# A second Strassen level for two of the seven products of an MLP's second matmul

## Chip, cores, metric

One Trainium2 chip, one core. The metric is the device time of one execution in microseconds (us), the median of several.

## The reference

```python
B, S, D, F = 1, 2048, 1024, 3584            # bf16 inputs
def reference(x, w1, b1, w2, b2):
    y = _layernorm(x, axis=-1)
    h = _gelu(jnp.einsum("bsd,df->bsf", y, w1) + b1)      # first matmul
    return jnp.einsum("bsf,fd->bsd", h, w2) + b2          # second matmul
```

## The kernel before

Tokens are worked in two blocks of 1024. In each, both matmuls are done by one level of Strassen's method (Winograd's form): operands are cut into quarters, seven products of quarters replace eight, and sums of quarters are made on VectorE (DVE). The program is made by a small list scheduler: it places every operation on its engine by an assumed cost and a priority, and so fixes each engine's in-order instruction stream before the kernel runs.

In the second matmul the quarters of `h` are A11 to A22 (512 tokens by 1792 of K), those of `w2` are B11 to B22 (1792 by 512 columns). S and T are sums of them. One product is four token tiles, each of 14 matmuls (128 of K, 128 tokens, 512 columns).

```python
SEQ2 = (1, 2, 5, 3, 6, 7, 4)
hold = {1: hb, 6: hb, 7: hb, 4: hb, 2: h2, 5: h5, 3: h5}     # PSUM banks, four each
...
def prods(p, a, b):
    first = prev[p] is None
    for t in range(TH):                                      # 4 token tiles
        fn = [(lambda e, k=k, t=t: e.matmul(
            ps[:, hold[p][t].k, :], lhsT=a[0][:, k, t * P:(t + 1) * P], rhs=b[0][:, k, :],
            start=(first and k == 0), stop=(k == NU - 1), skip_group_check=True), a[1][k] + b[1][k])
            for k in range(NU)]                              # 14 matmuls of 512 columns
        ...
        if p in (1, 5, 6):
            keep(p, t, 0 if p == 1 else 1, at)               # bank + bias -> SBUF (fp32)
        if p == 2:
            final(2, t, 11, 1, at, (h2[t],))                 # bank + kept 1 -> output quarter 11
        if p == 6:
            final(3, t, 12, 6, at + 1, (h5[t],))
        if p == 7:
            final(7, t, 22, 5, at, ())
        if p == 4:
            final(4, t, 21, None, at, (hb[t],))              # bank + bias -> output quarter 21
...
S1 = sums(s, h[21], A[21], A[22], ALU.add, (), pt[2], "hS1")
T1 = sums(s, w2q16[12], B[12], B[11], ALU.subtract, (), pt[2] + 4, "wT1")
prods(1, A[11], B[11])
S2 = sums(...)
prods(2, A[12], B[21])
...                                                          # products 5, 3, 6, 7 and their sums
prods(4, A[22], T4)
```

Of the kernel before, what the change touches and what calls it, by code (L numbers as in the profile page):

```python
# [23 lines left out]
P = 128  # L24
HT = 512
# [9 lines left out]
MM512 = 0.2163  # L35
MM256 = 0.1085
# [8 lines left out]
class Op:  # L45
# [3 lines left out]
    def __init__(self, engs, cost, fn, deps, prio, name, sem=None, inc=1, nbytes=None, alloc=None, frees=()):  # L49
# [3 lines left out]
        self.sem, self.inc, self.nbytes, self.alloc, self.frees = sem, inc, nbytes, alloc, frees  # L53
# [20 lines left out]
class Planner:  # L74
# [12 lines left out]

    def place(self):
# [12 lines left out]
        while left:  # L101
            best = None
            for e in self.ENGS:
                cands = []
                t0 = 1e9
                for o in avail:
# [3 lines left out]
                    if o.alloc is not None:  # L110
                        fr = o.alloc.pool.free
                        if not fr:
                            continue
                        rel = fr[0][1]
                        if rel is not None:
                            r = max(r, rel.end + LAT)
# [15 lines left out]
            if o.alloc is not None:  # L132
                k, rel = o.alloc.pool.free.pop(0)
                o.alloc.k = k
                if rel is not None:
                    o.deps.append(rel)
            c = o.cost[e] if isinstance(o.cost, dict) else o.cost
# [59 lines left out]
def bass_standalone__mixer_channel_mlp__prompt_kernel(  # L197
# [24 lines left out]
    with ExitStack() as es:  # L222
# [25 lines left out]
        x16 = x_sb[:, :, :].bitcast(FP16)  # L248
        h = {q: h_sb[:, n] for n, q in enumerate((11, 12, 21, 22))}
        w2a16 = w2a_sb[:, :, :, :].bitcast(FP16)  # L250
# [21 lines left out]
        T_MM2 = TH * 7 * NU * MM512  # L272
# [314 lines left out]
        KG = [(k, min(k + 2, NU)) for k in range(0, NU, 2)]  # L587
        w2_free = {}
        stores = []
        SLOT2 = NU * MM512  # L590
        SEQ2 = (1, 2, 5, 3, 6, 7, 4)

        def sums(s, dst, a, b, op, deps, prio, name):

            res = []
            for g, (k0, k1) in enumerate(KG):
                dl = list(deps)
                for k in range(k0, k1):
                    dl += a[1][k] + b[1][k]
                o = add("DVE", 0.63, lambda e, k0=k0, k1=k1: e.tensor_tensor(  # L600
                    out=dst[:, k0:k1, :], in0=a[0][:, k0:k1, :], in1=b[0][:, k0:k1, :], op=op),
                    list(dict.fromkeys(dl)), prio + 0.3 * g, f"{name}_{s}_{g}")
# [3 lines left out]
        def flat(a):  # L606
            return list(dict.fromkeys(o for l in a[1] for o in l))

        def mm2_block(s):
            t0 = base2[s]  # L610
            pt = {p: t0 + k * TH * SLOT2 for k, p in enumerate(SEQ2)}
            m2, rd, sn = {}, {}, {}
            hb = [Holder(banks) for _ in range(TH)]
            h2 = [Holder(banks) for _ in range(TH)]
            h5 = [Holder(banks) for _ in range(TH)]
            hold = {1: hb, 6: hb, 7: hb, 4: hb, 2: h2, 5: h5, 3: h5}
            prev = {1: None, 2: None, 5: None, 6: 1, 7: 6, 4: 7, 3: 5}
# [3 lines left out]
            def done(p):  # L621
                return [m2[(p, t)] for t in range(TH)]

            def evac(p, t, dst, in1, deps, name, at, alloc, frees):
                return add("DVE", 0.69, lambda e: e.tensor_tensor(out=dst(), in0=ps[:, hold[p][t].k, :], in1=in1(),  # L625
                                                                  op=ALU.add), [m2[(p, t)], *deps], at,
                           f"{name}_{s}_{t}", alloc=alloc, frees=frees)
# [3 lines left out]

            def keep(p, t, d, at):
                hs = sn[(p, t)] = Holder(snaps)
                rd[(p, t)] = evac(p, t, lambda: sn_sb[:, hs.k, :], bias(d), (b2_ld,), f"r{p}", at, hs, ())

            def final(p, t, q, add_p, at, frees):
                ho = Holder(outs)
                r = (s * NT + (q // 10 - 1) * TH + t) * P
                c = (q % 10 - 1) * HT
                if add_p is None:  # L640
                    in1, deps = bias(0), (b2_ld,)
                else:
                    hs = sn[(add_p, t)]
                    in1, deps, frees = (lambda: sn_sb[:, hs.k, :]), (rd[(add_p, t)],), (hs, *frees)
                f = rd[(p, t)] = evac(p, t, lambda: o_sb[:, ho.k, :], in1, deps, f"o{q}", at, ho, frees)
# [4 lines left out]
            def prods(p, a, b):  # L650
                first = prev[p] is None
                for t in range(TH):
# [12 lines left out]
                    if p == 2:  # L665
                        final(2, t, 11, 1, at, (h2[t],))
# [129 lines left out]
```

## Time and profile before

| | before |
|---|---|
| median of 3 runs | 357.11 us (356.89 to 358.32) |
| span of the profiled run | 355.3 us |
| TensorE (PE) busy | 347.8 us, 98% |
| VectorE (DVE) busy | 236.1 us, 66% |
| granted TensorE clock, mean | 0.999 |

PE is busy 98% of the span. This alone proves little: the Trainium skill, Perfetto Trace Analysis, "Identifying the Most-Contended Engine", says that matmul busy time is no good measure of headroom. Stronger evidence is that the chain of waits, followed back from the end, never leaves PE in the body. These are its pieces from the first second-matmul block on (start, length, what; "x49" are recorded matmuls, of which a few per cent are missing):

```profile
98.63 10.74 PE ps L653 x49
...
109.42 10.74 PE ps L653 x49
...
120.21 14.62 PE ps L653 x67
...
183.18 84.61 PE ps L533 x392
...
267.84 10.74 PE ps L653 x49
...
314.89 37.52 PE ps L653 x173
352.41 0.02 issue
352.44 0.69 DVE o_sb L625
```

The second-matmul block from 267.84 to 352.44 is 84.6 us for 392 matmuls: 215.9 ns each, with no stall. The next view, the busy table by windows, takes product 1, product 2 and the whole second block. Its columns are the window, its length, then busy us (and instructions) of PE, weight loads, DVE, ScalarE and GpSimd, then clock, DMA share and GB/s:

```profile
98.60:110.70 12.10, 12.02 (x55) 5.46 (x56) 5.06 (x8) 1.03 (x2) 0.00 (x0) 1.00 1.07 346
110.70:122.80 12.10, 12.05 (x56) 5.47 (x56) 9.42 (x17) 0.00 (x0) 0.00 (x0) 1.00 0.23 73
267.90:352.40 84.50, 84.29 (x387) 38.02 (x390) 48.60 (x77) 0.94 (x2) 0.00 (x0) 1.00 0.21 67
```

DVE is busy 5.06 of 12.1 us in product 1, 9.42 in product 2 and 48.60 of 84.5 us in the block, so there seems to be room. The timeline of PE in the head (start, length, line, operation, count) becomes important later:

```profile
6.50 1.03 PE L401 MATMUL ps<-ident,x_sb 128*128 128x128 f16 x8 [2.50 <-DVE x_sb L363]
8.11 1.86 PE L495 MATMUL ps<-yw_sb,w_sb 128*128 128x128 f16 x16 [0.58 <-ACT yw_sb L408]
9.77 0.72 PE L401 MATMUL ps<-ident,x_sb 128*128 128x128 f16 x8
10.32 1.06 PE L495 MATMUL ps<-yw_sb,w_sb 128*128 128x128 f16 x16
```

Eight 128-column matmuls (transposes) take 1.03 us, then 0.72; sixteen take 1.86 us, then 1.06. The array starts at half its clock here: eight like them take 0.62 us later in the head. The mean of 0.999 and the sliced clock row of the page do not show it, because they count the time before the first clock record of the trace as full clock. The first full-width products on `t1` operands start at 28.48 us.

### The profile page before, as it was taken

The numbers are of one execution on the slowest core, as the hardware profiler recorded it, in microseconds if no ns is written. First come the engines' busy times: TensorE is split into PE (matmuls) and PEld (weight loads), VectorE is DVE, ScalarE is ACT, GpSimd is POOL, SyncE is SP. The second block draws the span as 40 slices with busy tenths as digits, with TensorE's granted clock in tenths as the row PEclk, the third lists the DMA queues.
The fourth block names the chain that finished last, engine by engine and source line by source line (L and its number), as shares of the span: only waits on it lengthen the run. The fifth ranks groups of instructions, "written<-read, shape, count | busy, mean of one in ns | idle before, by whom it ended". The sixth has DMA issues, their size and how long they took to land.

```text
span 355.3 us, 4675 instructions
## 1 busy us (share of the span) xinstructions
PE 347.8 (98%) x1833; PEld 168.5 (47%) x1843; DVE 236.1 (66%) x395; ACT 125.7 (35%) x202; POOL 12.1 (3%) x31
## 2 busy tenths in 40 slices
PE   5999999999999999999999999999999999999996
PEld 4985444444444444444444444444444444444442
DVE  5789799898847658972716657655542946797222
ACT  4766766577620000000017676667662000000000
POOL 2310000010100000000000000000000000000000
PEclk9999999999999999999999999999999999999999
DMA  7739849643096100155765333030007510001111
GB/s 247 243 58 345 267 118 326 209 118 100 21 316 217 45 14 2 34 114 93 224 220 156 109 118 111 11 117 2 0 1 248 167 44 17 0 0 45 45 44 44
DMA packets 47391, 40.93 MB, mean 115 GB/s; under 512 B 12298, under 2 KB 45322, under 8 KB 47370
## 3 DMA queue, kind: packets, MB, share of 16 engines
q1 hardware_dynamic: 47226, 40.52, 37.2%
q8 instruction: 14, 0.23, 0.3%
q10 hardware_dynamic: 144, 0.13, 0.1%
q14 instruction: 7, 0.06, 0.1%
HBM read 33.82 MB, written 4.19 MB: 107 GB/s over the span
## 4 chain that ended last, share of the span: by engine, by line
PE 97%; DMA 1%; ACT 1%; issue 0%; SPq 0%; DVE 0%
PE ps L653 47%; PE ps L533 44%; PE ps L495 4%; DMA x_sb<-in_x_dram 1%; PE ps L401 1%; ACT h_sb L372 0%; SPq L278 0%; DVE o_sb L625 0%; ACT yw_sb L408 0%; ACT mv_sb L374 0%; PE ps L341 0%
## 5 line engine op out<-in xcount | busy, mean ns | idle before, releaser
L653 PE MATMUL ps<-w2a_sb,h_sb 128*128 128x512 bf16 (+1 forms) x442 | 96.7, 379 | 0.3
L533 PE MATMUL ps<-yw_sb,t_sb 128*128 128x512 f16 x416 | 96.2, 379 | 0.0
L545 ACT COPY sn_sb<-ps 128x512 f32<-128x512 f32 x67 | 39.2, 585 | 105.5 <-PE ps L533 105.5
L533 PE MATMUL ps<-yw_sb,w_sb 128*128 128x512 f16 x312 | 73.9, 379 | 0.0
L653 PE MATMUL ps<-yw_sb,h_sb 128*128 128x512 f16 (+1 forms) x332 | 72.6, 379 | 0.2
L653 PEld LDWEIGHTS ps<-w2a_sb,h_sb 128*128 128x128 f16 x448 | 43.7, 98 | 52.9
L556 ACT ACTIVATE h_sb<-sn_sb,b_sb 128x512 f16<-128x512 f32 x78 | 55.2, 718 | 24.2 <-DVE sn_sb L550 19.9
L533 PEld LDWEIGHTS ps<-yw_sb,t_sb 128*128 128x128 f16 x416 | 40.6, 98 | 49.0
L550 DVE TENSOR_TENSOR sn_sb<-ps,sn_sb 128x512 f32<-128x512 f32 x78 | 52.4, 687 | 14.9 <-PE ps L533 14.2
L653 PEld LDWEIGHTS ps<-yw_sb,h_sb 128*128 128x128 f16 x336 | 32.8, 98 | 39.7
L533 PEld LDWEIGHTS ps<-yw_sb,w_sb 128*128 128x128 bf16 x312 | 30.3, 98 | 36.6
L600 DVE TENSOR_TENSOR h_sb<-h_sb 128x1024 f16<-128x1024 f16 x56 | 35.8, 683 | 2.4 <-ACT h_sb L556 2.4
L625 DVE TENSOR_TENSOR sn_sb<-ps,b_sb 128x512 f32<-128x512 f32 x24 | 16.6, 690 | 25.4 <-PE ps L653 25.4
L625 DVE TENSOR_TENSOR o_sb<-ps,sn_sb 128x512 bf16<-128x512 f32 x24 | 16.6, 691 | 24.7 <-PE ps L653 24.5
L470 DVE TENSOR_TENSOR t_sb<-w_sb,t_sb 128x1024 f16<-128x1024 bf16 x26 | 17.9, 689 | 11.9 <-PE ps L533 11.2
L470 DVE TENSOR_TENSOR t_sb<-w_sb 128x1024 f16<-128x1024 bf16 x26 | 17.8, 683 | 10.6 <-PE ps L533 8.3
L353 DVE BATCH_NORM_STATS2 st_sb<-x_sb 128x6 f32<-128x512 bf16 x26 | 17.3, 679 | 4.4 <-DMA x_sb<-in_x_dram 4.4
L556 ACT ACTIVATE h_sb<-ps,b_sb 128x512 f16<-128x512 f32 x26 | 17.7, 682 | 1.9 <-PE ps L533 1.9
L495 PE MATMUL ps<-yw_sb,w_sb 128*128 128x128 f16 x256 | 16.4, 225 | 0.6 <-ACT yw_sb L408 0.6
L495 PEld LDWEIGHTS ps<-yw_sb,w_sb 128*128 128x128 bf16 x256 | 15.4, 100 | 1.3 <-DMA w_sb<-in_w_dram 0.8
L625 DVE TENSOR_TENSOR o_sb<-ps,b_sb 128x512 bf16<-128x512 f32 x8 | 5.5, 690 | 14.0 <-PE ps L653 14.0
L437 DVE TENSOR_TENSOR yw_sb<-yw_sb 128x1024 f16<-128x1024 f16 x16 | 9.9, 686 | 0.3 <-PE ps L495 0.2
(37 smaller groups left out, 101.8 us busy)
## 6 DMA issues: line engine op xcount, KB each, us to landing
w_sb<-in_w_dram SPq DMA_DIRECT2D x28, 512.0 KB, 5.0
w2a_sb<-in_w_dram SPq DMA_DIRECT2D x4, 1792.0 KB, 8.4
yw_sb<-in_w_dram SPq DMA_DIRECT2D x4, 1792.0 KB, 11.9
out_dram<-o_sb SPq DMA_DIRECT2D x32, 128.0 KB, 1.7
x_sb<-in_x_dram SPq DMA_DIRECT2D x15, 256.0 KB, 8.2
yw_sb<-x_sb SPq DMA_TRANSPOSE x20, 2.5
b_sb<-in_b_dram SPq DMA_DIRECT2D x1, 256.0 KB, 6.4
x_sb<-in_x_dram ACTq DMA_DIRECT2D x1, 128.0 KB, 2.5
```

The costliest lines, as they stand in the source:

```text
L353: st = [add("DVE", 0.68, lambda e, k=k: e.bn_stats(st_sb[:, i, 6 * k:6 * k + 6], x_sb[:, i, k * HT:(k + 1) * HT]), (x_ld[(s, i)][k], *gate ...
L401: fn = [(lambda e, j=j, k=k, hold=hold: e.transpose(out=ps16[:, hold.k, j * P:(j + 1) * P], in_=x16[:, i, k * HT + j * P:k * HT + (j + 1) ...
L437: res.append(add("DVE", 0.64, lambda e, sl=sl: e.tensor_tensor(out=yop[n][:, sl, :], in0=yop[x0][:, sl, :], in1=yop[x1][:, sl, :], op=op), ...
L470: return add("DVE", 0.65, lambda e: e.tensor_tensor(out=tv(k), in0=x0, in1=x1, op=ALU.subtract), [*deps, *war.get(k, ())], prio + 0.5 * k, ...
L495: fn = [(lambda e, b=b, hb=hold[f], f=f, k=k, t=t: e.matmul(ps[:, hb.k, t * P:(t + 1) * P], lhsT=lhs[:, k, f * P:(f + 1) * P], rhs=yop[f"A ...
L533: fn = [(lambda e, k=k: e.matmul(ps[:, hold[p].k, :], lhsT=lhs[:, k, :], rhs=yop[yo][:, k, :], start=(first and k == 0), stop=(k == KH - 1 ...
L545: return e.copy(out=dst, in_=src) if o_.eng == "ACT" else e.tensor_copy(dst, src)
L550: return add("DVE", 0.69, lambda e: e.tensor_tensor(out=sn_sb[:, hold_s.k, :], in0=ps[:, hold[p].k, :], in1=sn_sb[:, hold_s.k, :], op=ALU. ...
L556: r = h_ok[(s, q, u)] = add("ACT", 0.70, lambda e: e.activation(out=h[q][:, u, :], in_=src(), func=ACT.Gelu_apprx_tanh, bias=b1_sb[:, f:f ...
L600: o = add("DVE", 0.63, lambda e, k0=k0, k1=k1: e.tensor_tensor(out=dst[:, k0:k1, :], in0=a[0][:, k0:k1, :], in1=b[0][:, k0:k1, :], op=op), ...
L625: return add("DVE", 0.69, lambda e: e.tensor_tensor(out=dst(), in0=ps[:, hold[p][t].k, :], in1=in1(), op=ALU.add), [m2[(p, t)], *deps], at ...
L653: fn = [(lambda e, k=k, t=t: e.matmul(ps[:, hold[p][t].k, :], lhsT=a[0][:, k, t * P:(t + 1) * P], rhs=b[0][:, k, :], start=(first and k == ...
```

## The change

A12 B21 and A22 T4 each enter one output quarter only (so does product 3, which stays as it was). The change runs each of the two by Strassen's method once more: halves of tokens (256), of K (896) and of columns (256), seven sub-products of 14 matmuls of 256 columns, in the order 1, 5, 6, 2, 7, 3, 4. Intent: 7/8 of the columns for these products. The price is eight more operand sums per product on DVE, written into buffers that are idle at that time, and evictions in pairs of half-width pieces. As A22 T4 can no longer accumulate on product 7's bank, product 7 is evicted twice. Sub-products 6, 7 and 4 accumulate on the bank of 1, and 3 on that of 5, and so wait for the eviction before them. The scheduler's assumed matmul costs are set to 0.2159 and 0.1092 us (0.2163 and 0.1085 before). The loads of the next block's `w1` move behind A12 B21.

```diff
-        T_MM2 = TH * 7 * NU * MM512
+        T_MM2 = TH * 5 * NU * MM512 + 2 * 7 * NU * MM256
...
+        INNER = (2, 4)
+        KI = NU // 2
+        HI = HT // 2
...
-                    if p == 2:
-                        final(2, t, 11, 1, at, (h2[t],))
...
-                        final(7, t, 22, 5, at, ())
-                    if p == 4:
-                        final(4, t, 21, None, at, (hb[t],))
+                        final(7, t, 22, 5, at, (hb[t],), kept=True)
...
+            def inner(p, a, b, xb, yb, war, q, add_p):
...
+                s1 = tt(xb[0], X["21"], X["22"], ALU.add, 5, "S1")
+                t1 = tt(yb[0], Y["12"], Y["11"], ALU.subtract, 5, "T1")
+                s2 = tt(xb[1], s1, X["11"], ALU.subtract, 6, "S2")
+                t2 = tt(yb[1], Y["22"], t1, ALU.subtract, 6, "T2")
...                                                     (s3, t3, s4, t4)
+                def sub(r, deps):
+                    x, y = opn[r]
+                    first = r in (1, 2, 5)
+                    fn = [(lambda e, k=k, j=j: e.matmul(
+                        ps[:, bank[r].k, j * HI:(j + 1) * HI], lhsT=x[0][:, k, j * P:(j + 1) * P], rhs=y[0][:, k, :],
+                        start=(first and j == k == 0), stop=(k == KI - 1), skip_group_check=True), x[1][k] + y[1][k])
+                        for j in range(2) for k in range(KI)]
...
+                sub(1, ())
+                kept(1, 0, 0, k1)
+                sub(5, ())
+                kept(5, 1, 1, k5)
+                sub(6, (ev[1],))
+                kept(6, 0, 1, k2, (r_[0], r_[1]))
+                sub(2, ())
+                outp(2, 0, 0, k1, (c2, k1), True)
+                sub(7, (ev[6],))
+                outp(7, 1, 1, k5, (k5,), True)
+                sub(3, (ev[5],))
+                outp(3, 0, 1, k2, (c5, k2))
+                sub(4, (ev[7],))
+                outp(4, 1, 0, None, (c0, r_[2], r_[3]))
+                for t in range(TH):
+                    store(q, t, ho[t], (ev[2], ev[3]) if t < 2 else (ev[7], ev[4]), at[3 if t < 2 else 4] + SUB)
...
-            prods(2, A[12], B[21])
+            inner(2, A[12], B[21], xb, yb, list(dict.fromkeys(ring)), 11, 1)
...
-            prods(4, A[22], T4)
+            inner(4, A[22], T4, halves(h_flat[12]), halves(h_flat[11]), done(3) + done(6) + flat(S4, S3), 21, 7)
```

More of the change, by code (lines that the diff above doesn't have):

```diff
@@ L33 @@
 DMA_T = (4, 6)
-MM512 = 0.2163
-MM256 = 0.1085
+MM512 = 0.2159
+MM256 = 0.1092
 MM128 = 0.0562
@@ L52, in __init__ @@
         self.deps = [d for d in deps if d is not None]
-        self.sem, self.inc, self.nbytes, self.alloc, self.frees = sem, inc, nbytes, alloc, frees
+        self.sem, self.inc, self.nbytes, self.frees = sem, inc, nbytes, frees
+        self.alloc = () if alloc is None else alloc if isinstance(alloc, tuple) else (alloc,)
         self.eng = None
@@ L86, in add, with take @@
         return o
+    @staticmethod
+    def take(alloc):
+        n, res = {}, []
+        for h in alloc:
+            i = n.get(id(h.pool), 0)
+            if i >= len(h.pool.free):
+                return None
+            res.append(h.pool.free[i])
+            n[id(h.pool)] = i + 1
+        return res
     def place(self):
@@ L109, in place @@
                     r = max(o.ready, free[e])
-                    if o.alloc is not None:
-                        fr = o.alloc.pool.free
-                        if not fr:
-                            continue
-                        rel = fr[0][1]
+                    slots = self.take(o.alloc)
+                    if slots is None:
+                        continue
+                    for _, rel in slots:
                         if rel is not None:
@@ L131, in place @@
             o.start = r
-            if o.alloc is not None:
-                k, rel = o.alloc.pool.free.pop(0)
-                o.alloc.k = k
+            for h, (k, rel) in zip(o.alloc, self.take(o.alloc)):
+                h.k = k
                 if rel is not None:
                     o.deps.append(rel)
+            for h in o.alloc:
+                h.pool.free.pop(0)
             c = o.cost[e] if isinstance(o.cost, dict) else o.cost
@@ L248, in bass_standalone__mixer_channel_mlp__prompt_kernel @@
         x16 = x_sb[:, :, :].bitcast(FP16)
+        w1_16 = w1_sb[:, :, :, :].bitcast(FP16)
         h = {q: h_sb[:, n] for n, q in enumerate((11, 12, 21, 22))}
+        h_flat = {q: t.rearrange("p u n -> p (u n)") for q, t in h.items()}
         w2a16 = w2a_sb[:, :, :, :].bitcast(FP16)
@@ L584, in mm1_unit, with sums @@
             return list(mine.values())
-        KG = [(k, min(k + 2, NU)) for k in range(0, NU, 2)]
         w2_free = {}
-        stores = []
         SLOT2 = NU * MM512
         SEQ2 = (1, 2, 5, 3, 6, 7, 4)
-        def sums(s, dst, a, b, op, deps, prio, name):
+        INNER = (2, 4)
+        KI = NU // 2
+        HI = HT // 2
+        def sums(dst, a, b, op, deps, prio, name, step=2, cost=0.63):
             res = []
-            for g, (k0, k1) in enumerate(KG):
+            n = len(a[1])
+            for g, k0 in enumerate(range(0, n, step)):
+                k1 = min(k0 + step, n)
                 dl = list(deps)
@@ L599, in sums, with flat @@
                     dl += a[1][k] + b[1][k]
-                o = add("DVE", 0.63, lambda e, k0=k0, k1=k1: e.tensor_tensor(
+                o = add("DVE", cost * (k1 - k0) / step, lambda e, k0=k0, k1=k1: e.tensor_tensor(
                     out=dst[:, k0:k1, :], in0=a[0][:, k0:k1, :], in1=b[0][:, k0:k1, :], op=op),
-                    list(dict.fromkeys(dl)), prio + 0.3 * g, f"{name}_{s}_{g}")
+                    list(dict.fromkeys(dl)), prio + 0.15 * step * g, f"{name}_{g}")
                 res += [[o]] * (k1 - k0)
             return dst, res
-        def flat(a):
-            return list(dict.fromkeys(o for l in a[1] for o in l))
+        def flat(*a):
+            return list(dict.fromkeys(o for x in a for l in x[1] for o in l))
         def mm2_block(s):
             t0 = base2[s]
-            pt = {p: t0 + k * TH * SLOT2 for k, p in enumerate(SEQ2)}
+            pt = {}
+            for p in SEQ2:
+                pt[p] = t0
+                t0 += 7 * NU * MM256 if p in INNER else TH * SLOT2
             m2, rd, sn = {}, {}, {}
             hb = [Holder(banks) for _ in range(TH)]
-            h2 = [Holder(banks) for _ in range(TH)]
             h5 = [Holder(banks) for _ in range(TH)]
-            hold = {1: hb, 6: hb, 7: hb, 4: hb, 2: h2, 5: h5, 3: h5}
-            prev = {1: None, 2: None, 5: None, 6: 1, 7: 6, 4: 7, 3: 5}
+            hold = {1: hb, 6: hb, 7: hb, 5: h5, 3: h5}
+            prev = {1: None, 5: None, 6: 1, 7: 6, 3: 5}
             A = {q: (h[q], [[h_ok[(s, q, u)]] for u in range(NU)]) for q in h}
@@ L621, in done @@
             def done(p):
-                return [m2[(p, t)] for t in range(TH)]
-            def evac(p, t, dst, in1, deps, name, at, alloc, frees):
-                return add("DVE", 0.69, lambda e: e.tensor_tensor(out=dst(), in0=ps[:, hold[p][t].k, :], in1=in1(),
-                                                                  op=ALU.add), [m2[(p, t)], *deps], at,
-                           f"{name}_{s}_{t}", alloc=alloc, frees=frees)
+                return m2[p] if p in INNER else [m2[(p, t)] for t in range(TH)]
@@ L629, in bias, with plus, whole @@
+            def plus(out, bank, x):
+                return lambda e: e.tensor_tensor(out=out(), in0=bank(), in1=x(), op=ALU.add)
             def bias(d):
                 return lambda: b2_sb[:, d * HT:(d + 1) * HT]
+            def whole(t, h_):
+                return lambda: t[:, h_.k, :]
             def keep(p, t, d, at):
                 hs = sn[(p, t)] = Holder(snaps)
-                rd[(p, t)] = evac(p, t, lambda: sn_sb[:, hs.k, :], bias(d), (b2_ld,), f"r{p}", at, hs, ())
-            def final(p, t, q, add_p, at, frees):
-                ho = Holder(outs)
+                rd[(p, t)] = add("DVE", 0.69, plus(whole(sn_sb, hs), whole(ps, hold[p][t]), bias(d)),
+                                 (m2[(p, t)], b2_ld), at, f"r{p}_{s}_{t}", alloc=hs)
@@ L638, in final, with store @@
+            def store(q, t, ho, deps, at):
                 r = (s * NT + (q // 10 - 1) * TH + t) * P
                 c = (q % 10 - 1) * HT
-                if add_p is None:
-                    in1, deps = bias(0), (b2_ld,)
-                else:
-                    hs = sn[(add_p, t)]
-                    in1, deps, frees = (lambda: sn_sb[:, hs.k, :]), (rd[(add_p, t)],), (hs, *frees)
-                f = rd[(p, t)] = evac(p, t, lambda: o_sb[:, ho.k, :], in1, deps, f"o{q}", at, ho, frees)
-                o = add("SP", 0.42, lambda e: e.dma_start(of[r:r + P, c:c + HT], o_sb[:, ho.k, :]), (f,), at + 0.5,
-                        f"st{q}_{s}_{t}", sem=ho, inc=16, nbytes=P * HT * 2, frees=(ho,))
@@ L648, in final @@
-                stores.append(o)
+                add("SP", 0.42, lambda e: e.dma_start(of[r:r + P, c:c + HT], o_sb[:, ho.k, :]), deps, at + 0.5,
+                    f"st{q}_{s}_{t}", sem=ho, inc=16, nbytes=P * HT * 2, frees=(ho,))
+            def final(p, t, q, add_p, at, frees, kept=False):
+                ho, hs = Holder(outs), sn[(add_p, t)]
+                bank = whole(ps, hold[p][t])
+                fn = [(plus(whole(o_sb, ho), bank, whole(sn_sb, hs)), ())]
+                alloc = (ho,)
+                if kept:
+                    hk = sn[(p, t)] = Holder(snaps)
+                    fn.append((plus(whole(sn_sb, hk), bank, bias(0)), ()))
+                    alloc += (hk,)
+                f = rd[(p, t)] = add("DVE", 0.65 * len(fn), fn, (m2[(p, t)], rd[(add_p, t)], b2_ld), at,
+                                     f"o{q}_{s}_{t}", alloc=alloc, frees=(hs, *frees))
+                store(q, t, ho, (f,), at)
@@ L669, in prods @@
                     if p == 7:
-                        final(7, t, 22, 5, at, ())
-                    if p == 4:
-                        final(4, t, 21, None, at, (hb[t],))
-            S1 = sums(s, h[21], A[21], A[22], ALU.add, (), pt[2], "hS1")
-            T1 = sums(s, w2q16[12], B[12], B[11], ALU.subtract, (), pt[2] + 4, "wT1")
-            prods(1, A[11], B[11])
-            S2 = sums(s, h[11], S1, A[11], ALU.subtract, done(1), pt[5] - 2, "hS2")
-            prods(2, A[12], B[21])
-            S4 = sums(s, h[12], A[12], S2, ALU.subtract, done(2), pt[3] - 8, "hS4")
+                        final(7, t, 22, 5, at, (hb[t],), kept=True)
@@ new lines, in inner, with tt, part, kept @@
+            def inner(p, a, b, xb, yb, war, q, add_p):
+                nm = f"{p}_{s}"
+                X = {f"{i + 1}{j + 1}": (a[0][:, j * KI:(j + 1) * KI, i * HI:(i + 1) * HI], a[1][j * KI:(j + 1) * KI])
+                     for i in range(2) for j in range(2)}
+                Y = {f"{i + 1}{j + 1}": (b[0][:, i * KI:(i + 1) * KI, j * HI:(j + 1) * HI], b[1][i * KI:(i + 1) * KI])
+                     for i in range(2) for j in range(2)}
+                SUB = 2 * KI * MM256
+                at = {r: pt[p] + k * SUB for k, r in enumerate(SEQ1)}
+                def tt(dst, x, y, op, r, n):
+                    return sums(dst, x, y, op, war, at[r] - 3 * SUB, f"i{n}_{nm}", step=4, cost=0.62)
+                s1 = tt(xb[0], X["21"], X["22"], ALU.add, 5, "S1")
+                t1 = tt(yb[0], Y["12"], Y["11"], ALU.subtract, 5, "T1")
+                s2 = tt(xb[1], s1, X["11"], ALU.subtract, 6, "S2")
+                t2 = tt(yb[1], Y["22"], t1, ALU.subtract, 6, "T2")
+                s3 = tt(xb[2], X["11"], X["21"], ALU.subtract, 7, "S3")
+                t3 = tt(yb[2], Y["22"], Y["12"], ALU.subtract, 7, "T3")
+                s4 = tt(xb[3], X["12"], s2, ALU.subtract, 3, "S4")
+                t4 = tt(yb[3], Y["21"], t2, ALU.subtract, 4, "T4")
+                opn = {1: (X["11"], Y["11"]), 2: (X["12"], Y["21"]), 3: (s4, Y["22"]), 4: (X["22"], t4), 5: (s1, t1),
+                       6: (s2, t2), 7: (s3, t3)}
+                c0, c2, c5 = Holder(banks), Holder(banks), Holder(banks)
+                bank = {1: c0, 6: c0, 7: c0, 4: c0, 2: c2, 5: c5, 3: c5}
+                k1, k2, k5 = Holder(snaps), Holder(snaps), Holder(snaps)
+                ho = [Holder(outs) for _ in range(TH)]
+                subs, ev = {}, {}
+                def part(t, h_, j):
+                    return lambda: t[:, h_.k, j * HI:(j + 1) * HI]
+                def sub(r, deps):
[5 more added lines that the diff above has]
+                        for j in range(2) for k in range(KI)]
+                    subs[r] = add("PE", SUB, fn, list(dict.fromkeys([*deps] + [d for _, l in fn for d in l])), at[r],
+                                  f"M{p}{r}_{s}", alloc=bank[r] if first else None)
+                def kept(r, i, j, hs, frees=()):
+                    fn = [(plus(part(sn_sb, hs, v), part(ps, bank[r], v), part(sn_sb, sn[(add_p, 2 * i + v)], j)), ())
+                          for v in range(2)]
+                    ev[r] = add("DVE", 0.68, fn, (subs[r], *(rd[(add_p, 2 * i + v)] for v in range(2))), at[r] + SUB,
+                                f"k{p}{r}_{s}", alloc=hs, frees=frees)
+                def outp(r, i, j, hs, frees, alloc=False):
+                    src = [part(sn_sb, sn[(add_p, 2 * i + v)], j) if hs is None else part(sn_sb, hs, v)
+                           for v in range(2)]
+                    fn = [(plus(part(o_sb, ho[2 * i + v], j), part(ps, bank[r], v), src[v]), ()) for v in range(2)]
+                    k = {2: 1, 7: 5, 3: 6}.get(r)
+                    ev[r] = add("DVE", 0.68, fn, [subs[r]] + ([ev[k]] if k else []), at[r] + SUB, f"o{p}{r}_{s}",
+                                alloc=tuple(ho[2 * i:2 * i + 2]) if alloc else None, frees=frees)
+                r_ = [sn[(add_p, t)] for t in range(TH)]
+                sub(1, ())
[14 more added lines that the diff above has]
+                    store(q, t, ho[t], (ev[2], ev[3]) if t < 2 else (ev[7], ev[4]), at[3 if t < 2 else 4] + SUB)
+                m2[p] = list(subs.values()) + flat(s1, s2, s3, s4, t1, t2, t3, t4)
@@ new lines, in halves @@
+            def halves(t):
+                return [t[:, r * KI * HI:(r + 1) * KI * HI].rearrange("p (k n) -> p k n", n=HI) for r in range(4)]
+            n = s * NC + NC - 1
+            ring = [o for m in range(n - 2, n + 1) for o in w1_use[m]]
+            ring += [o for m in (n - 1, n) for l in t1_use[m].values() for o in l]
+            xb = halves(t1_sb[:, :, :, :, :].rearrange("p a b k c -> p (a b k c)"))
+            yb = halves(w1_16[:, :, :, :].rearrange("p a k c -> p (a k c)"))
+            S1 = sums(h[21], A[21], A[22], ALU.add, (), pt[5] - 12, f"hS1_{s}")
@@ new lines, in mm2_block @@
+            T1 = sums(w2q16[12], B[12], B[11], ALU.subtract, (), pt[5] - 8, f"wT1_{s}")
+            prods(1, A[11], B[11])
+            S2 = sums(h[11], S1, A[11], ALU.subtract, done(1), pt[5] - 2, f"hS2_{s}")
+            inner(2, A[12], B[21], xb, yb, list(dict.fromkeys(ring)), 11, 1)
+            for m in range(n - 2, n + 1):
+                w1_use[m] = w1_use[m] + done(2)
+            for m in (n - 1, n):
+                for k in range(1, 5):
+                    t1_use[m][k] = t1_use[m].get(k, []) + done(2)
@@ L680, in mm2_block @@
+            S4 = sums(h[12], A[12], S2, ALU.subtract, done(2), pt[3] - 8, f"hS4_{s}")
             prods(5, S1, T1)
-            T2 = sums(s, w2q16[12], B[22], T1, ALU.subtract, done(5), pt[6] - 10, "wT2")
+            T2 = sums(w2q16[12], B[22], T1, ALU.subtract, done(5), pt[6] - 10, f"wT2_{s}")
             prods(3, S4, B[22])
-            S3 = sums(s, h[21], A[22], S2, ALU.subtract, done(5), pt[7] - 12, "hS3")
-            T3 = sums(s, w2q16[11], T2, B[11], ALU.subtract, done(1), pt[7] - 8, "wT3")
@@ L685, in mm2_block @@
-            T4 = sums(s, w2q16[21], B[21], T2, ALU.subtract, done(2), pt[4] - 8, "wT4")
+            S3 = sums(h[21], A[22], S2, ALU.subtract, done(5), pt[7] - 12, f"hS3_{s}")
+            T3 = sums(w2q16[11], T2, B[11], ALU.subtract, done(1), pt[7] - 8, f"wT3_{s}")
+            T4 = sums(w2q16[21], B[21], T2, ALU.subtract, done(2), pt[4] - 14, f"wT4_{s}")
             prods(6, S2, T2)
             prods(7, S3, T3)
-            prods(4, A[22], T4)
-            w2_free[s] = {22: done(3) + flat(T2), 12: done(6) + flat(T3) + flat(T4), 11: done(7), 21: done(4)}
@@ L690, in mm2_block @@
-            hf = {11: done(6) + flat(S4) + flat(S3), 12: done(3), 21: done(7), 22: done(4) + flat(S3)}
+            inner(4, A[22], T4, halves(h_flat[12]), halves(h_flat[11]), done(3) + done(6) + flat(S4, S3), 21, 7)
+            w2_free[s] = {22: done(3) + flat(T2), 12: done(6) + flat(T3, T4), 11: done(7), 21: done(4)}
+            hf = {11: done(4), 12: done(4), 21: done(7), 22: done(4) + flat(S3)}
             for q in h:
@@ L720, in bass_standalone__mixer_channel_mlp__prompt_kernel @@
                 m = n + N_W1
-                if m < NSB * NC:
-                    load_w1(m // NC, m % NC, t0 + 14 * SLOT)
+                if m < (s + 1) * NC:
+                    load_w1(s, m % NC, t0 + 14 * SLOT)
                 if s == 0 and c == 2:
@@ L729, in bass_standalone__mixer_channel_mlp__prompt_kernel @@
             if s + 1 < NSB:
+                for c in range(N_W1):
+                    load_w1(s + 1, c, base2[s] + 40 + c)
                 wf = w2_free[s]
```

## The prediction

> **What bounds the kernel now.** TensorE. The page's busy table has PE 98%, VectorE (DVE) 66%, ScalarE 35%; the chain of waits is 97% PE; the granted clock is 0.999. In the timeline, 8 matmuls of 512 columns start every 1.727 us, 215.9 ns each; each second-matmul block (392 of them) takes 84.6 us, 98.5 to 183.0 and 267.8 to 352.4, without a stall. Only fewer PE columns help, if nothing else starts to be waited for.
>
> **Removed, added, moved.** Each of the four rerouted products (two per block) has 56 matmuls of 512 columns: 56 x 215.9 ns = 12.09 us. It becomes 7 x 14 = 98 of 256. No trace line has that width, but the head has 80 matmuls of 128 columns, each with its weight load, in 4.46 us, 55.7 ns apart: the weight load does not set the pace even there. The line through 55.7 and 215.9 gives 109.1 ns (estimate). The Trainium skill, TensorE: Matmul & The Clock Gate, "Wait — 56ns, not 53.3ns?", has N/2.4 GHz + about 2.5 ns, so 109.2; the trace agrees at 128 and 512. Hence 10.70 us, 1.39 us saved each, 5.55 us in all, 1.55%. That is the ceiling.
>
> DVE pays. Per rerouted product: eight operand sums of 1792 elements in two instructions (0.60 + about 0.47 us; the timeline repeats a 128x1024 sum every 0.60): 8.5 us; seven evictions as pairs of 128x256, about 0.34 us each against 0.61 for 128x512 (estimate): 4.8 us; for A22 T4 also four extra 128x512 copies, 2.4 us; four evictions of 0.61 go. Net 11 to 13 us each, +48 us: DVE from 236 to about 285 us, 81%; nearly full around the inner products.
>
> **On the critical path?** I walked the DVE order against PE's by these durations. Inner A12 B21: the sums start when the first-matmul block ends; with the evictions they are about 12.9 us of work against the 12.1 us of product 1, but only the first pair is needed 1.5 us after that. One sub-product (1.53 us) lies between a sub-product and the one that accumulates on its bank; the pair eviction takes about 0.8, so it fits if DVE is at most 0.5 us late. The w1 prefetch that shared the queues with the w2 load at 98 us moves later, so the w2 quarter should land 7.3 us after the block's start, as in the second block (275.1), not 10.5. Inner A22 T4 of the first block competes with 4.9 us of next-block sums (they wait for transposes), but PE interleaves next-block matmuls. I expect 0 to 1 us of new PE waits, about 0.2.
>
> Tail: the last pair costs about 0.77 us against 0.69, and two stores (0.33 to 0.42 us each to issue) wait for it: +0.5 us.
>
> **Prediction:** 357.1 - 5.55 + 0.5 + 0.2 = 352.2 us; 8 in 10: 351.4 to 353.7. Faster by over 2%: 0.03; within: 0.95; slower: 0.02.
>
> **What would show it.** Matmuls of 256 columns 109 ns apart; inner products 10.7 us; second block about 81.8 us; PE idle inside blocks under 1 us; DVE about 285 us busy; span near 350.5.
>
> **What would make it wrong.** A 256-column matmul slower because of its weight load (at 123 ns the saving is gone); DVE late in an inner chain, so that PE waits for sums or bank evictions; evictions dearer than 0.34 us; late transposes holding DVE's in-order queue; first-matmul blocks disturbed by the changed DVE order.

## The result, and the profile after

| | before | changed |
|---|---|---|
| median (4 runs each, same chip) | 357.72 us | 353.13 us (353.04 to 353.43) |
| ratio | 1 | 0.9872, 95% interval 0.9842 to 0.9903 |
| span of the profiled run | 355.3 us | 351.6 us |
| PE busy | 347.8 us, 98% | 343.6 us, 98% |
| DVE busy | 236.1 us, 66% | 284.8 us, 81% |

A ratio here is the mean time of one kernel's fast runs over the mean of the other's in the same rounds, so it is not quite the ratio of the medians. The change makes the kernel 1.3% faster: within 2%, as predicted, and inside the predicted range.

The chain of waits, second-matmul blocks (the inner products are the pieces of line L733):

```profile
99.90 10.74 PE ps L681 x49
110.64 0.05 issue
110.69 1.24 PE ps L681 x5
111.93 9.17 PE ps L733 x84
...
266.33 10.74 PE ps L681 x49
...
277.13 1.24 PE ps L681 x5
278.37 9.17 PE ps L733 x84
...
337.41 10.71 PE ps L733 x98
348.13 0.02 issue
348.15 0.42 DVE o_sb L645
348.57 0.33 DVEq L235
```

The second block is now 266.33 to 348.15: 81.8 us, 2.8 us less, as predicted. From the first block's start to the second's it is 166.4 us against 169.2 before, again 2.8 us. PE does not wait inside the blocks: the only waits that the profile gives PE are three in the head, which the kernel before has as well. The same windows, and product 7 as well (158.7 to 170.8):

```profile
99.90:111.80 11.90, 11.85 (x55) 5.42 (x56) 11.75 (x21) 0.99 (x2) 0.00 (x0) 1.00 0.97 309
111.80:122.50 10.70, 10.70 (x93) 8.93 (x92) 10.17 (x24) 0.00 (x0) 0.00 (x0) 1.00 0.05 16
158.70:170.80 12.10, 12.10 (x57) 5.49 (x56) 11.96 (x22) 0.00 (x0) 0.00 (x0) 1.00 0.56 108
266.30:348.10 81.80, 81.61 (x472) 46.37 (x474) 72.06 (x132) 1.03 (x2) 0.00 (x0) 1.00 0.20 65
```

The cost is in the column of DVE: it goes from 5.06 to 11.75 us in the 11.9 us of product 1 and is full in product 7 (11.96 of 12.10). The first block as a whole is tighter than the second: from 99.9 to 183.0 us DVE is busy 80.17 of 83.1 us, against 72.06 of 81.8. The weight loads (the column before) rise from 5.47 to 8.93 us in the window that holds most of the rerouted product, because its 98 matmuls need 98 loads instead of 56; PE shows no wait for them. (The scheduler places the last 14 of these matmuls a little later, behind 14 of product 5.) The timeline of PE in the inner product shows the pace: each 14 matmuls of 256 columns start 1.53 us after the 14 before, and the chain above has 84 in 9.17 us, 109.2 ns each.

```profile
111.77 1.69 PE L733 MATMUL ps<-w2a_sb,h_sb 128*128 128x256 bf16 x14
...
116.35 1.69 PE L733 MATMUL ps<-w2a_sb,h_sb 128*128 128x256 bf16 x14
117.88 1.69 PE L733 MATMUL ps<-w2a_sb,t_sb 128*128 128x256 bf16 x14
119.41 1.69 PE L733 MATMUL ps<-w_sb,t_sb 128*128 128x256 f16 x14
```

In the head the changed kernel's profile is later than that of the kernel before:

```profile
6.51 1.03 PE L416 MATMUL ps<-ident,x_sb 128*128 128x128 f16 x8 [2.51 <-DVE x_sb L378]
8.12 1.86 PE L510 MATMUL ps<-yw_sb,w_sb 128*128 128x128 f16 x16 [0.58 <-ACT yw_sb L423]
9.78 1.06 PE L416 MATMUL ps<-ident,x_sb 128*128 128x128 f16 x8
10.63 1.91 PE L510 MATMUL ps<-yw_sb,w_sb 128*128 128x128 f16 x16
...
29.75 0.59 PE L548 MATMUL ps<-yw_sb,t_sb 128*128 128x512 f16 x2
```

The second eight transposes (9.78) and the next sixteen matmuls (10.63) still run at half clock, where the kernel before went to full clock. The clock records in the two traces say the same: full clock is granted from 9.99 us in the kernel before and from 12.96 us here. The first `t1` products start at 29.75 us instead of 28.48. So the account of the spans is 355.3 - 5.6 (blocks) + 0.6 (tail) + 1.3 (head) = 351.6. The 5.6 was predicted as 5.55 and the tail as 0.5; the 1.3 was not in the prediction. Experiments had to show whether it belongs to the change.

### The profile page after: what moved, and what is told of

Same layout as the page of the kernel before. It is cut to its first block, busy times and chain, and to the rows that moved or that the text cites. A ratio compares the mean times of both kernels' runs of the same rounds, so it can differ in the third digit from the quotient of the medians.

```text
span 351.6 us, 5124 instructions
## 1 busy us (share of the span) xinstructions
PE 343.6 (98%) x2003; PEld 186.5 (53%) x2011; DVE 284.8 (81%) x509; ACT 125.1 (36%) x200; POOL 12.1 (3%) x31
## 4 chain that ended last, share of the span: by engine, by line
PE 97%; DMA 1%; ACT 1%; SPq 0%; issue 0%; DVE 0%; DVEq 0%
PE ps L548 45%; PE ps L681 34%; PE ps L733 12%; PE ps L510 5%; DMA x_sb<-in_x_dram 1%; PE ps L416 1%; ACT h_sb L387 0%; SPq L293 0%; ACT yw_sb L423 0%; DVE o_sb L645 0%; DVEq L235 0%; ACT mv_sb L389 0%; PE ps L356 0%
## 5 line engine op out<-in xcount | busy, mean ns | idle before, releaser
L560 ACT COPY sn_sb<-ps 128x512 f32<-128x512 f32 x65 | 38.1, 586 | 103.0 <-PE ps L548 103.0
L548 PEld LDWEIGHTS ps<-yw_sb,w_sb 128*128 128x128 bf16 x312 | 30.4, 98 | 36.0
L681 PE MATMUL ps<-w2a_sb,h_sb 128*128 128x512 f16 (+1 forms) x220 | 48.5, 379 | 0.2
L618 DVE TENSOR_TENSOR h_sb<-h_sb 128x1024 f16<-128x1024 f16 x72 | 45.2, 667 | 0.0
L681 PEld LDWEIGHTS ps<-w2a_sb,h_sb 128*128 128x128 f16 x224 | 21.9, 98 | 26.4
L645 DVE TENSOR_TENSOR sn_sb<-ps,b_sb 128x512 f32<-128x512 f32 x32 | 21.9, 685 | 6.9 <-PE ps L681 6.9
L645 DVE TENSOR_TENSOR o_sb<-ps,sn_sb 128x256 bf16<-128x256 f32 (+1 forms) x48 | 23.0, 507 | 5.5 <-PE ps L733 4.5
L510 PE MATMUL ps<-yw_sb,w_sb 128*128 128x128 f16 x256 | 17.3, 230 | 0.6 <-ACT yw_sb L423 0.6
L733 PE MATMUL ps<-w2a_sb,h_sb 128*128 128x256 f16 (+1 forms) x140 | 16.9, 273 | 0.0
L510 PEld LDWEIGHTS ps<-yw_sb,w_sb 128*128 128x128 bf16 x256 | 16.2, 104 | 1.3 <-DMA w_sb<-in_w_dram 0.8
L733 PEld LDWEIGHTS ps<-w2a_sb,h_sb 128*128 128x128 f16 x140 | 13.7, 98 | 2.7
```

What stands on the lines that cost most here:

```text
L510: fn = [(lambda e, b=b, hb=hold[f], f=f, k=k, t=t: e.matmul(ps[:, hb.k, t * P:(t + 1) * P], lhsT=lhs[:, k, f * P:(f + 1) * P], rhs=yop[f"A ...
L548: fn = [(lambda e, k=k: e.matmul(ps[:, hold[p].k, :], lhsT=lhs[:, k, :], rhs=yop[yo][:, k, :], start=(first and k == 0), stop=(k == KH - 1 ...
L560: return e.copy(out=dst, in_=src) if o_.eng == "ACT" else e.tensor_copy(dst, src)
L618: o = add("DVE", cost * (k1 - k0) / step, lambda e, k0=k0, k1=k1: e.tensor_tensor(out=dst[:, k0:k1, :], in0=a[0][:, k0:k1, :], in1=b[0][:, ...
L645: return lambda e: e.tensor_tensor(out=out(), in0=bank(), in1=x(), op=ALU.add)
L681: fn = [(lambda e, k=k, t=t: e.matmul(ps[:, hold[p][t].k, :], lhsT=a[0][:, k, t * P:(t + 1) * P], rhs=b[0][:, k, :], start=(first and k == ...
```

## The experiments

Theory: the change is worth exactly its PE columns minus a longer tail, DVE just keeps up, and the head is chance. Rivals: the change delays the head; weight loads or DVE eat part of the gain; DVE's 19% of idle time is real room.

This table of all profiles serves several experiments. "t1" is the start of the first `t1` products; "rest" is the span less that; "tail" is from the start of the last eviction to the end. Groups are the first two runs of eight transposes and the first two of sixteen matmuls in the head, by their lengths in us.

| run | 8, 16, 8, 16 | t1 | span | rest | tail |
|---|---|---|---|---|---|
| before | 1.03, 1.86, 0.72, 1.06 | 28.48 | 355.3 | 326.8 | 2.9 |
| changed, first profile | 1.03, 1.86, 1.06, 1.91 | 29.75 | 351.6 | 321.8 | 3.4 |
| n1_again (changed) | 0.62, 1.87, 1.06, 1.37 | 29.07 | 350.9 | 321.8 | 3.4 |
| n2_again (changed) | 0.62, 1.86, 1.06, 1.50 | 28.62 | 350.4 | 321.8 | 3.4 |
| e1, only A12 B21 | 0.62, 1.86, 1.06, 1.40 | 29.14 | 353.2 | 324.1 | 2.9 |
| e2, only A22 T4 | 1.03, 1.89, 1.06, 1.91 | 30.00 | 354.8 | 324.8 | 3.5 |
| e3, tail split | 1.04, 1.87, 0.68, 1.06 | 28.36 | 349.6 | 321.2 | 2.9 |
| w1, warm start | 0.62, 1.07, 0.62, 1.07 | 29.57 | 351.4 | 321.8 | 3.4 |
| w2, before, warm start | 0.62, 1.05, 0.61, 1.06 | 28.62 | 355.5 | 326.9 | 2.9 |
| w3, tail split, warm start | 0.62, 1.05, 0.62, 1.06 | 29.38 | 350.7 | 321.3 | 2.9 |
| b1, the same again | 0.62, 1.05, 0.61, 1.06 | 28.84 | 350.1 | 321.3 | 2.9 |

### The changed kernel again (n1_again)

No edit.

> The changed kernel, unaltered, run again. Theory: the 1.27 us that its profile loses before the first full-width block (first 512-column block of t1 products starts at 29.75 us, before 28.48) is a phase of the TensorE clock in the head, not the change: this profile may show either about 28.5 or about 29.8, the second-matmul blocks again 81.8 us (second one) and the tail again 3.5 us after the last matmul. Rival: the change itself delays the head: 29.8 again in every profile of the changed kernel and its variants. Ratio to before 0.986 +- 0.003.

Measured: 352.68 us against 357.95 us (six runs against eleven), ratio 0.9851 (0.9827 to 0.9874). The `t1` products start at 29.07, which is neither of the two values that were expected but lies between them; the rest is 321.8 us again. Over all profiles in the table the head varies from 28.4 to 30.0 us, while kernels with equal bodies agree in the rest to 0.1 us. Only two of these profiles are of the kernel before, so the table alone would not exclude a small delay by the change. The clock records and the times of the kernel before, below, show where the variation comes from; no sign of a delay by the change is left.

### One product at a time (e1_only_a12b21, e2_only_a22t4)

Edit: the old path of products 2 and 4 is put back beside the new one, and only one of them takes the inner level.

```diff
-            inner(2, A[12], B[21], ...)
+            if 2 in INNER:
+                inner(2, A[12], B[21], ...)
+            else:
+                prods(2, A[12], B[21])
```

(The same for product 4; product 7 is evicted twice only where product 4 is inner.)

> Only A12 B21 runs by the inner level, A22 T4 as before. If the gain is columns alone: two products x 1.39 us = 2.78 us saved, no tail cost, so about 0.7 percent faster than before (ratio 0.992), second block 84.6 - 1.39 = 83.2 us, tail 2.9 us. If the inner sums that must run while product 1 runs make TensorE wait, the saving is smaller and PE shows waits at the start of the inner product.

> Only A22 T4 runs by the inner level. Columns alone: 2.78 us saved, minus the longer tail of 0.6 us: 2.2 us, ratio 0.994; second block 83.2 us, tail 3.5 us. A rival that puts the tail's 0.6 us on the run and not on the pair eviction with two stores would show a tail of 2.9 us here.

Measured: A12 B21 alone gives 355.02 us, ratio 0.9927 (0.9900 to 0.9954); the rest is 2.7 us shorter than before, tail 2.9 us. A22 T4 alone gives 356.29 us, 0.9957 (0.9935 to 0.9978); the rest is 2.0 us shorter, tail 3.5 us. Its second block, 268.13 to 351.33, is 83.2 us as expected. So both parts save their columns, the tail's 0.6 us belongs to A22 T4 standing last, and the two add up to 4.7 us against 5.0 us for both together. The missing 0.2 us of e2 lies in its first block: there the weight load of the last sub-product (186.08 us) waited for the eviction of sub-product 7, with 4 other matmuls between them where the changed kernel has 8, and PE lost 0.15 us.

### The tail (e3_tail_split)

Edit: only in the last inner product, the two token tiles of the chain 1, 6, 7, 4 use two banks, and sub-product 4 is two operations, each with its own eviction and store. Two banks are needed: the Trainium skill, PSUM — Partial Sum Buffer, "PSUM bank collisions raise a hardware error", rules out that DVE reads a bank that PE is writing.

```diff
-                sub(4, (ev[7],))
-                outp(4, 1, 0, None, (c0, r_[2], r_[3]))
+                for v in range(2):              # token tile v: 7 matmuls, eviction, store
+                    m = add("PE", SUB / 2, fn, ...)                   # into bank[4][v]
+                    f = add("DVE", 0.42, plus(part(o_sb, ho[2 + v], 0), part(ps, bank[4][v], v), ...), (m, ev[7]), ...)
+                    store(q, 2 + v, ho[2 + v], (ev[7], f), ...)
```

> The changed kernel with only its very last sub-product altered: its two token tiles are accumulated in two banks, each half is evicted by itself (the first while TensorE still works on the second) and stored as soon as it is complete. Theory: the tail after the last matmul falls from 3.5 us to about 2.6 us (one 128x256 eviction of 0.42 and one store instead of a pair of 0.76 and two stores), so 0.85 us less than the changed kernel: ratio to before about 0.984. If the tail stays at 3.5 us, the two stores or evictions are not its cause.

Measured: 352.65 us, ratio 0.9849 (0.9824 to 0.9874); in the times it does not stand apart from the changed kernel in the same rounds (352.68 us), because the head scatters more than this. In the trace it does: the rest is 321.2 us instead of 321.8. The ends of both timelines, first the changed kernel (the last eviction pair, then two stores issued after 348.9), then the split tail:

```profile
346.62 0.76 DVE L645 TENSOR_TENSOR o_sb<-ps,sn_sb 128x256 bf16<-128x256 f32 x2 [0.77 <-PE ps L733]
347.40 2.33 SPq L661 DMA_DIRECT2D out_dram<-o_sb  x4
348.15 0.75 DVE L645 TENSOR_TENSOR o_sb<-ps,sn_sb 128x256 bf16<-128x256 f32 x2 [0.77 <-PE ps L733]
```

```profile
345.22 1.19 DVE L645 TENSOR_TENSOR o_sb<-ps,sn_sb 128x256 bf16<-128x256 f32 x3 [0.77 <-PE ps L735]
346.01 1.80 SPq L661 DMA_DIRECT2D out_dram<-o_sb  x4
346.75 0.42 DVE L645 TENSOR_TENSOR o_sb<-ps,sn_sb 128x256 bf16<-128x256 f32 x1 [0.34 <-PE ps L760]
```

The last eviction is one of 0.42 us instead of a pair of 0.75. The tail fell by 0.6 us to 2.9, not by 0.85 to 2.6 as expected: pair and stores together are the cause of the longer tail (this run does not part them), but the shorter eviction did not bring it below that of the kernel before. The single records of the trace say why: the last eviction ends at 347.18, but the last store is issued only at 347.35, after the issue of the store before it has ended (347.31), and it lands 1.83 us later, against 1.70 us for the last store of the kernel before. These two delays, 0.15 and 0.13 us, use up the 0.27 us that the eviction saved.

### The head: clock or transfer (w1_warm56, w2_before_warm56)

Edit, in each kernel:

```diff
-N_WARM = 26
+N_WARM = 56
```

These are the idle matmuls on a block of ones that the kernel runs at the start. The Trainium skill, TensorE: Matmul & The Clock Gate, "What's actually happening", says that the array is at half clock by default and goes to full clock once an activity window of about 3.4 us, which runs freely and does not start with the kernel, has been busy. The traces agree. In seven profiles without the edit, the second sixteen matmuls take anything from 1.06 to 1.91 us. Their clock records change only in steps of 3.413 us: full clock lasts 344.75 us in the kernel before, 337.92 in the changed kernel and 341.33 in e3, which are 101, 99 and 100 such steps, and n1, n2 and e1 each have one step at half clock in the head, from 7.9, 7.6 and 8.0 us.

> The changed kernel with 56 instead of 26 idle matmuls on a block of ones at the very start, to keep TensorE busy from 1.0 us to the first transposes at 6.5 us. Theory: the start of the first full-width products (t1 operands) varied from 28.4 to 30.0 us over six profiles because the first 128-column matmuls run at half clock until a phase of the clock that differs from run to run; kept busy, the array is at full clock from the first real matmul, so 8 transposes take 0.6 and 16 matmuls about 1.0 us, the t1 products start at 28.3 us or before, and runs scatter less: about 1 us less than the changed kernel, ratio to before about 0.983. Rival (transfers, not the clock, set the head): no change of the head, 28.4 to 30.

> The kernel before with the same 56 starting matmuls. If the head is a matter of the clock and not of the change, this gains as much as the changed kernel does from it, about 0.5 to 1 us (ratio 0.998), and the t1 products start at 28.3 us or earlier. If it gains nothing while the changed kernel does, the head's delay belongs to the change.

Measured: the kernel before gains, 357.23 us, ratio 0.9975 (0.9957 to 0.9993), and its six runs lie within 0.35 us (357.12 to 357.47), while eleven runs without the edit spread from 356.86 to 358.94. Its `t1` products start at 28.62 us, not at 28.3 or earlier as expected. The half clock costs the kernel before just as well, and was most of its scatter: a step at half clock lowers the mean clock by about 0.005, and in the two batches that have runs listed at 0.99, that is with two such steps, these are its slowest (359.35 and 359.03 us; 358.94 us). The changed kernel's first matmuls are at full clock too (table), with 352.67 us and 0.9834 (0.9810 to 0.9859). This interval overlaps those of the changed kernel (0.9851 and 0.9874), which was not run in the same rounds, and the runs still scatter by 1.55 us (351.58 to 353.13); so no gain of the warm start is shown for it by itself. Its `t1` products start at 29.57 us in the profile. There the seventh tile of x landed late. ScalarE waited 3.06 us for it, against 0.72 us in the kernel before (first fence: before; second: warm start):

```profile
14.72 1.06 ACT L372 ACTIVATE h_sb<-x_sb 128x1024 f16<-128x1024 bf16 x1 [0.72 <-DMA x_sb<-in_x_dram]
```

```profile
16.49 1.06 ACT L387 ACTIVATE h_sb<-x_sb 128x1024 f16<-128x1024 bf16 x1 [3.06 <-DMA x_sb<-in_x_dram]
```

So half of my expectation failed, the earlier start and the smaller scatter. The head has two run-to-run causes, the clock's phase and the landing of x. ScalarE starts on that tile at 16.3 and 16.5 us in two of the warm profiles (w1, w3), and between 13.7 and 15.4 us in all others; taking one cause away lets the other be the limit. Whether the late landing in those two is chance or has to do with the edit is open.

### Is VectorE's idle time room? (d1_sums_twice)

Edit: each inner operand sum is done a second time, with the same result, as an operation that the scheduler takes for free.

```diff
                 o = add("DVE", cost * (k1 - k0) / step, ...)
+                if step == 4:
+                    o = add("DVE", 0.0, o.fn, [o], ...)
```

> The changed kernel with every inner operand sum done twice (the same result), 8.5 us more VectorE work per inner product, 34 us in all. Theory: VectorE is nearly full around the inner products although it is busy only 81% of the span, so TensorE must wait: the block with A12 B21 has 12.9 us of VectorE work against 12.1 us of product 1, so I expect 5 to 8 us of PE waits in each inner A12 B21, less in A22 T4, and 10 to 25 us in all, slower than before (ratio 1.01 to 1.05). Rival (VectorE has 19% free, 67 us, and the sums are off the chain): under 2 us of waits, ratio below 0.995.

Measured: 383.42 us, ratio 1.0698 (1.0668 to 1.0728): 7% slower than before and about 30 us above the changed kernel's 352.7 to 353.1 us, for 34 us more DVE work (284.8 to 318.5 us busy). The direction is the theory's; my size of 10 to 25 us was too small for the time. PE's waits, and PE's timeline around the first:

```profile
PE ps L735 <- DVE sn_sb L647: 18.7, 4, 5.3
...
PE ps L735 <- DVE o_sb L647: 1.4, 1, 1.4
...
PE ps L548 <- DVE yw_sb L452: 1.0, 1, 1.0
PE ps L735 <- DVE h_sb L618: 0.8, 2, 0.4
```

```profile
111.76 1.69 PE L735 MATMUL ps<-w_sb,t_sb 128*128 128x256 f16 x14
118.74 3.17 PE L735 MATMUL ps<-w_sb,t_sb 128*128 128x256 f16 x14 [5.29 <-DVE sn_sb L647]
121.69 2.07 PE L735 MATMUL ps<-w2a_sb,h_sb 128*128 128x256 bf16 x14
123.60 1.69 PE L735 MATMUL ps<-w2a_sb,t_sb 128*128 128x256 bf16 x14
```

Sub-product 6 waits 5.29 us for the eviction of 1, which stands behind sums in DVE's instruction stream. Then its 14 matmuls take 3.17 us instead of 1.69: the array is at half clock (granted clock 0.50 from 115.7 to 122.4 us), which my expectation left out. The waits inside the body add up to 21.9 us, within the 10 to 25 us. Most of the other 8 us is the half clock: the records have three such stretches of 6.8 us, and half of PE's busy time in them (3.66, 3.70 and 5.70 us) is 6.5 us (estimate). So the cost is not simply the added DVE time. The order may play a part as well: the scheduler took the second sums for free and could not arrange the evictions around them, and no run tried another order. But the two blocks have only 2.9 and 9.7 us of idle DVE time, for 34 us of work whose results are due in them. 81% busy means here: full where it matters.

### What hides the eviction (o1_chain_adjacent)

Edit, in the last inner product only (the condition that says so is left out here): order 1, 6, 5, 2 instead of 1, 5, 6, 2.

```diff
-                sub(5, ())
-                kept(5, 1, 1, k5)
                 sub(6, (ev[1],))
                 kept(6, 0, 1, k2, (r_[0], r_[1]))
+                sub(5, (subs[6],))
+                kept(5, 1, 1, k5)
-                sub(2, ())
+                sub(2, (subs[5],))
```

> The changed kernel, with the order of the very last inner product changed: sub-products 1, 6, 5, 2 instead of 1, 5, 6, 2, so that 6, which accumulates on 1's bank after its eviction, follows 1 at once. Theory: sub-product 5 in between (1.53 us) is what hides the eviction pair; without it TensorE waits for the pair, 0.76 us, plus VectorE's lateness there (0.2 us in the changed kernel's trace): about 1.0 us of PE wait, at one place only, and a second-matmul block of 82.8 us instead of 81.8. Rival (the accumulation does not wait, or VectorE evicts during the sub-product): no wait, 81.8 us.

Measured in its trace:

```profile
336.79 1.69 PE L733 MATMUL ps<-w2a_sb,h_sb 128*128 128x256 f16 x14
339.33 3.23 PE L733 MATMUL ps<-h_sb 128*128 128x256 f16 x28 [0.85 <-DVE sn_sb L645]
342.40 1.69 PE L733 MATMUL ps<-w2a_sb,h_sb 128*128 128x256 f16 x14
```

Sub-product 1 starts at 336.79 and lasts 1.53; sub-product 6 starts at 339.33, so it waited 1.0 us, at this one place. The second block is 82.8 us (265.88 to 348.69) instead of 81.8. Both as expected. After this short wait the next 28 matmuls take 3.23 us, full clock, unlike after the 5.29 us of the run before. The order 1, 5, 6, 2, 7, 3, 4 hides about 1 us at this place; the other places were not tried.

### The faster version (w3_tail_and_warm56, n2_again, b1_best_again)

Edit: the split tail and the 56 starting matmuls together.

> The changed kernel with the split tail of the earlier run and the 56 starting matmuls: both add, about 1.5 us less than the changed kernel, ratio to before about 0.982, and the least scatter. Nothing else in it moves: second block 81.8 us, tail 2.9 us.

> The changed kernel unaltered, as the partner of the next run on the same chip: ratio to before 0.986 +- 0.003; t1 products start anywhere from 28.2 to 30.0 us, from there to the end 321.8 us as in the two earlier profiles.

> Split tail and 56 starting matmuls again, beside the changed kernel on the same chip: from the start of the t1 products to the end 321.2 us (0.6 less than the changed kernel, the split tail), the head anywhere from 28 to 29.6 us because the seventh tile of x still lands when it lands; 0.5 to 1.2 us faster than the changed kernel in the median, which the intervals may not separate.

Measured first beside the two warm kernels: 352.01 us, 0.9833 (0.9809 to 0.9858), no better than the warm start alone (0.9834), and with one run at 353.48, so not the least scatter. Then beside the changed kernel on the same chip: 351.70 us (351.23 to 351.94) against 352.98 us (352.13 to 354.09), ratios to before 0.9833 (0.9819 to 0.9846) and 0.9874 (0.9854 to 0.9895). These intervals do not overlap: this version beats both kernels, the changed one by 1.3 us, a little more than expected. Its rest is 321.3 us, the changed kernel's 321.8, so 0.5 us of that is the tail. That the other part is the head is only a remainder: in the two profiles of these rounds its head is later (28.84 against 28.62 us).

## Why the prediction was right, point by point

- PE bound, and the gain is its columns: right. 5.55 us predicted, 5.6 us in the traces' blocks, repeated within 0.1 us in three profiles. 256-column matmuls start 109.2 ns apart (109.1 predicted), each with its own weight load. A rerouted product costs 10.7 instead of 12.09 us: 7/8 of the columns, times 218.4/215.9, since two narrow matmuls take 2.5 ns more than one wide one.
- DVE near its limit but not on the chain: right. 284.8 us busy against 285 predicted, no PE wait in the blocks (0.2 us was allowed). d1 and o1 show how thin this is: the sums twice cost 30 us (the half clock after the waits included), and one place without its spacer costs 1.0 us.
- The next block's `w1` load moved away from the `w2` load: half shown. The first `w2` quarter of the first block lands 7.3 us after its issue (99.88 to 107.19), as predicted, where the kernel before has 10.5 us (98.61 to 109.08). That PE would have waited without this is only argued, for no run put the load back.
- Tail: +0.5 predicted, +0.6 measured. e2 puts it on A22 T4, e3 on the pair and its two stores together.
- The sum: 352.2 predicted, 353.13 measured, inside the range and above its middle. Most of the difference of 0.9 us is the start of the sum: the prediction took 357.1, the median of three runs, and with a fourth run the kernel before has 357.72. Between the medians the gain is 4.6 us, where 4.85 was predicted. The term that the prediction did not have is behind both: the head, taken as equal, which was 1.27 us later in the profiled run of the changed kernel. It varies by up to 1.6 us between profiles, with the array's half-clock phase and with the landing of x. That a median of a few runs came so near is in part luck. The body's account was right within 0.2 us (rest: 322.0 predicted from 326.8 - 5.55 + 0.5 + 0.2, 321.8 measured).

## What to carry to other kernels

When one engine is on the chain for 97% of the time, a change is worth the work that it takes off that engine, computed from the start-to-start pace in the trace, plus what it does to the two ends; the middle then predicts itself. An off-chain engine's idle share is no measure of room: look at it in the windows where its results are due, and test it by adding work. For differences under 1 us, compare spans from a fixed event after the start, since a head that varies by more than that hides them in the times.

## What the Trainium skill lacked or had wrong

- TensorE: Matmul & The Clock Gate, "Back-to-back issue gap", gives a sustained pace in a stream of weight-load and matmul pairs of about 81 ns at 128 columns and about 131 ns at 512, and calls N/2.4 + 2.5 ns the isolated case. Here such streams run at 55.7 ns (128), 109.2 ns (256) and 215.9 ns (512): the formula holds in the stream, and the two sustained figures do not.
- The same page, "What's actually happening", describes the free-running window of about 3.4 us that sets the clock, and puts the cost of the ramp under 1% of a typical span. The runs agree: from none to over 1 us of 350. What it lacks is the spread in times that follows and a remedy: 2 us for one unchanged kernel, which shrank to 0.35 us with 30 more starting matmuls. Nor does it say that a mean clock can hide this: the profiles' means, that of d1 apart, are 0.995 to 1.0, and the one of 1.000 in e2 goes with the latest head of all; the lengths of the first matmuls show it.
- Perfetto Trace Analysis, "Identifying the Most-Contended Engine", takes weight-load busy share as a good measure of the distance to the roofline. Here it rose from 47% to 53% while the kernel got faster by doing less arithmetic: it followed the number of weight loads (1843 and 2011 records), so two kernels with matmuls of different widths can't be compared by it.
- Perfetto Trace Analysis, "Optimizing Scalar/DVE Operations", gives a busy overhead for each VectorE operation of about 60 ns on SBUF and 125 ns on PSUM. With the 0.96 GHz of VectorE: DVE Perf Modes, "Specifications", and one element per cycle, sums from PSUM would repeat every 0.66 us at 128x512 and 0.39 us at 128x256 (estimates). Here such a sum in fp32 repeats about every 0.61 us at 128x512 and 0.34 us at 128x256, nearer to the smaller overhead; one alone lasts 0.69 and 0.42 us. A pair of halves takes 0.67 us, 10% more than one whole.
